# A gated delta-rule and FFN kernel: the first FFN group in plain f32, chunks 0 and 1 re-blocked by VectorE transposes, and a new order of the work

## The chip, the core and the metric

The kernel runs on one core of one Trainium2 chip. The metric is device time in microseconds (us) of one execution. The core has TensorE (PE, with its weight load PEld), VectorE (DVE), ScalarE (ACT), GpSimd (POOL), and SyncE (SP), which issues the DMAs here.

## The reference

```python
def _attn_ref(q, k, v, beta):                 # (4, 8, 768, 48) each, beta (4, 8, 768)
    k_n = k / (np.linalg.norm(k, axis=-1, keepdims=True) + 1e-06)
    state = np.zeros((B, H, D, D))
    for t in range(S):
        kt, vt, bt = (k_n[:, :, t], v[:, :, t], beta[:, :, t, None])
        y[:, :, t] = np.einsum('bhd,bhde->bhe', q[:, :, t], state)
        v_old = np.einsum('bhde,bhd->bhe', state, kt)
        state = state + bt[:, :, :, None] * np.einsum('bhd,bhe->bhde', kt, vt - v_old)
    return y

def _moe_ref(x, w_in, w_out):                 # x (3072, 384), w_in (384, 2048), w_out (2048, 384)
    h = x @ w_in
    sp = np.maximum(h, 0.0) + np.log1p(np.exp(-np.abs(h)))
    g = h * erf(sp)
    return g @ w_out
```

The rows of x are the 3072 tokens of y. The weights arrive as double precision numbers; the core sees each as two 32-bit integers.

## The kernel before, in words

**The recurrence.** The 768 steps are cut into 12 chunks of 64. For each chunk the kernel forms the norms of k (`norms`, L245 to L258, 18 small VectorE steps for two chunks), the Gram matrices k·k and q·k on TensorE (`gram_mm`, L287 for chunks 0 and 1, L291 later), their scaled or masked copies A and pp (`gram_a` L301, `gram_p` L308), and the inverse of a triangular matrix per head. That inverse is built from 32x32 blocks. Two chunks are solved together: A is written to DRAM (`to_dram` L328), read back with one block per partition (`to_blocks` L337, tile gb), and forward substitution runs in 31 rows of two elementwise steps (`solve_row`, L355 and L357), for chunks 0 and 1 on VectorE and later on POOL. The result xb goes back to matrix form: for chunks 0 and 1 by 256 small TensorE products with an identity matrix (`back_t` L373) and copies (`back_x`), later over DRAM (`put_blocks`, `from_blocks`). The 32x32 halves are merged (`merge_t` L405, a VectorE transpose into T; `merge_e`, `merge_z`, `merge_m`), and a chain over the four batches updates the state and gives y (`chain_u` L485, `chain_u2` L491, `chain_s` L499, `chain_s2` L504, `chain_y` L511/L515, `chain_y2`, `chain_m` L526).

**The weights.** Each weight matrix is loaded in pieces of 512 columns (`w_load` L558; 512 KB each) and turned into f32: `w_mask` (ACT, L565), `w_sign` (L572), `w_bits` (VectorE, L579), with a running maximum `w_mx` (ACT L587, VectorE L590). From the maximum comes a power-of-two scale; then each f32 tile of 384 columns becomes two f16 halves: `w_hi` (ACT, L130) and `w_lo` (L649 on VectorE; for w_in by TensorE f32 products with a scaled identity, L641 and L642, and an ACT copy).

**The FFN.** One group is 256 tokens, one chunk of all four batches: 12 groups. x is scaled and split into f16 halves (`x_max` to `x_lo`, L658 to L685). For each of 16 tiles of d_ff, `ffn1` issues nine f16 products of 256 columns (L697). In units of two tiles, `e_sp` (Softplus, L719), `e_erf` (L724, each behind a load of ACT's function table, L165) and `e_mul` (L728, reads the products of L697 from PSUM, tile ph) make g, which `e_split` (L123 on ACT or L125) and `e_rest` (L118) split into halves; `ffn2` issues six f16 products of 384 columns per tile (L749 to L751). `ffn_out` and `ffn_store` scale and store.

**Order.** A program is recorded as a list of events; the tuple `ORDER` says in which order they are issued and `ENG` on which engine an event with a choice runs. Each engine runs its own instructions in that order, and DMAs are issued by SP in that order too. Matmuls on zeros (`warm` L180, `fill2` L186) are put between the real ones.

## Time and profile before

| | |
|---|---|
| three runs | 611.24, 614.84, 613.77 us; median 613.77 us |
| profiled execution | span 613.8 us from first to last instruction; its own time is taken as the same, since the run of 613.77 us agrees with it to the digits shown |
| busy PE / DVE / ACT / POOL | 97% / 66% / 85% / 50% of the span |
| mean granted TensorE clock | 0.983 |
| first / last FFN product | starts at 96.05 / ends at about 608.5 us |

The span falls into two parts. Up to 96 us the first two chunks are prepared and the weights are read; from then on FFN products are issued until 608.5 us, with the recurrence of later chunks between them. A busy PE includes the products on zeros, so its 97% is not 97% of needed work.

### The profile page before, as it was taken

To read this page: it belongs to the slowest core of one execution; us is meant where nothing else is said; L and a number is where in the kernel's file an instruction comes from. 1 tells how busy PE (TensorE), PEld (TensorE's weight loads), DVE (VectorE), ACT (ScalarE), POOL (GpSimd) and SP (SyncE) were. 2 spreads that over 40 slices of the span, in tenths; PEclk is the share of its full clock that TensorE was granted. 3 is DMA by queue.
4 is the path that set the end of the run, shared out by engine and by line. 5 is a ranking of instruction groups with operands and counts; after the bars stand their busy time and mean duration, and the time that the engine had idled before them with its cause. 6 is when DMAs were issued, how large, how long until landed. Compare 5 with 4: busy or idle time off the path is not lost.

```text
span 613.8 us, 25249 instructions
## 1 busy us (share of the span) xinstructions
PE 595.4 (97%) x11019; PEld 426.9 (70%) x11019; DVE 403.8 (66%) x926; ACT 522.9 (85%) x751; POOL 307.8 (50%) x484
## 2 busy tenths in 40 slices
PE   9899989999999899999999999999999999999996
PEld 3654456667777677777777777777777777777773
DVE  0769986668787788887776977666565655436221
ACT  8859897999996789878968999897989797989873
POOL 3000313798589733998527884489953122213221
PEclk9799898999999899999999999999999999999999
DMA  9999625850755367624485226713045200100111
GB/s 313 281 235 350 152 52 124 226 141 28 185 105 142 93 163 153 156 63 117 92 212 140 67 66 148 148 50 91 1 115 121 53 17 21 27 2 14 27 27 26
DMA packets 86382, 69.72 MB, mean 114 GB/s; under 512 B 64064, under 2 KB 73408, under 8 KB 86272
## 3 DMA queue, kind: packets, MB, share of 16 engines
q1 hardware_dynamic: 86272, 68.12, 43.1%
q8 instruction: 86, 1.41, 1.0%
q14 instruction: 24, 0.20, 0.1%
HBM read 48.17 MB, written 18.87 MB: 109 GB/s over the span
## 4 chain that ended last, share of the span: by engine, by line
PE 72%; POOL 7%; DVE 5%; DMA 5%; ACT 5%; issue 4%; SPq 1%; POOLq 0%; DVEq 0%; ACTq 0%
PE ph L697 25%; PE pr L749 9%; PE pr L751 9%; PE pr L750 9%; PE warm L180 3%; POOL xb L357 3%; POOL tmptmpg L355 2%; PE pc L485 2%; DMA qp<-qT 2%; PE pc L511 2%; PE pm L448 2%; DMA k<-ktok 2%; PE pc L515 2%; PE pc L499 2%; PE pg L291 1%
## 5 line engine op out<-in xcount | busy, mean ns | idle before, releaser
L165 ACT ACT_TABLE_LOAD x169 | 216.8, 1283 | 3.0
L697 PE MATMUL ph<-xh,w_in 128*128 128x256 f16 x1152 | 206.8, 274 | 0.1
L697 PEld LDWEIGHTS <-w_in 128*128 128x128 f16 x1728 | 166.5, 98 | 30.5 <-issue 2.2
L697 PE MATMUL ph<-xl,w_in 128*128 128x256 f16 x576 | 157.8, 274 | 1.2 <-DVE xl L685 1.2
L118 POOL TENSOR_TENSOR H<-L,H 128x512 f16<-128x512 f32 x58 | 69.3, 1203 | 134.6 <-DVE H L125 89.8
L749 PE MATMUL pr<-w_out,H 128*128 128x384 f16 x384 | 126.1, 328 | 0.0
L750 PE MATMUL pr<-w_out,H 128*128 128x384 f16 x384 | 125.7, 327 | 0.0
L751 PE MATMUL pr<-w_out,H 128*128 128x384 f16 x384 | 125.7, 327 | 0.0
L728 DVE SCALAR_TENSOR_TENSOR L<-ph,L 128x512 f32<-128x512 f32 x96 | 65.8, 687 | 88.9 <-ACT L L724 74.7
L118 POOL TENSOR_TENSOR z<-v,nm 64x192 f32<-64x192 f32 x94 | 51.8, 551 | 99.9 <-DMA v<-vtok 86.0
L357 POOL TENSOR_TENSOR xb<-xb,tmptmpg 128x31 f32<-128x31 f32 (+15 forms) x154 | 90.7, 589 | 12.1
L355 POOL TENSOR_TENSOR tmptmpg<-gb,xb 128x31 f32<-128x31 f32 (+15 forms) x154 | 83.6, 543 | 24.4 <-DMA gb<-d 11.2
L719 ACT ACTIVATE L<-ph,xct 128x512 f32<-128x512 f32 x96 | 65.4, 687 | 29.3 <-PE ph L697 25.9
L724 ACT ACTIVATE L<-L 128x512 f32<-128x512 f32 x96 | 59.9, 629 | 0.9
L751 PEld LDWEIGHTS <-H 128*128 128x128 f16 x384 | 37.6, 98 | 25.1 <-issue 0.2
L749 PEld LDWEIGHTS <-H 128*128 128x128 f16 x384 | 37.5, 98 | 22.8 <-issue 0.2
L750 PEld LDWEIGHTS <-H 128*128 128x128 f16 x384 | 37.6, 98 | 20.2 <-issue 0.2
L180 PE MATMUL warm<-zero 128*128 128x512 f16 x192 | 49.5, 412 | 1.2 <-DVE zero L171 1.2
L491 DVE TENSOR_TENSOR z<-pc,ga 64x192 f32<-64x192 f32 x88 | 31.2, 355 | 18.1 <-PE pc L485 16.4
L123 ACT CAST H<-L 128x512 f16<-128x512 f32 x56 | 33.5, 610 | 8.0 <-DVE L L728 7.9
L504 DVE TENSOR_TENSOR z<-pc,z 48x192 f32<-48x192 f32 x80 | 28.3, 353 | 17.3 <-PE pc L499 14.0
L180 PEld LDWEIGHTS <-zero 128*128 128x128 f16 x192 | 18.9, 104 | 25.6 <-issue 7.2
(159 smaller groups left out, 857.1 us busy)
## 6 DMA issues: line engine op xcount, KB each, us to landing
raw_in<-w_in SPq DMA_DIRECT2D x12, 512.0 KB, 7.1
raw_out<-w_out SPq DMA_DIRECT2D x12, 512.0 KB, 6.5
d<-A SPq DMA_DIRECT2D x22, 256.0 KB, 3.4
d<-pp SPq DMA_DIRECT2D x10, 512.0 KB, 3.7
qp<-d SPq DMA_DIRECT2D x20, 256.0 KB, 4.9
k<-ktok SPq DMA_DIRECT2D x12, 384.0 KB, 4.9
kpg<-kT SPq DMA_DIRECT2D x24, 192.0 KB, 4.5
qp<-qT SPq DMA_DIRECT2D x24, 192.0 KB, 3.6
```

The costliest lines, as they stand in the source:

```text
L118: {"V": ve, "G": ge}[pick(d)].tensor_tensor(*a, **kw)
L165: se.add_instruction(mybir.InstLoadActFuncSet(name=nc.get_next_instruction_name(), act_func_set_id=i, ins=[], outs=[]))
L180: te.matmul(wp[0], zero[:, :P], zero, start=True, stop=True)
L355: eng.tensor_tensor(tv, G[:, s, s + 1:].unsqueeze(1).broadcast_to([P, ncol, nr]), Xv[:, :, s:s + 1].broadcast_to([P, ncol, nr]), op=ALU.mult)
L357: eng.tensor_tensor(Xv[:, :, s + 1:], Xv[:, :, s + 1:], tv, op=ALU.add)
L697: te.matmul(ph, w[:, i, kt * P:kt * P + P], G[x][:, :, ksl], start=(m == 0), stop=(m == 8))
L719: se.activation(unit(g, u), G["ph", u], AF.Softplus, bias=0.0, scale=G["ct"])
L724: se.activation(Lu, Lu, AF.Erf, bias=0.0, scale=1.0)
L728: ve.scalar_tensor_tensor(Lu, fg[g]["ph", u], HSC, Lu, op0=ALU.mult, op1=ALU.mult)
L749: te.matmul(G["po"][a], gh[:, o, asl], wout_h[:, i, :], start=(i == 0), stop=False)
L750: te.matmul(G["po"][a], gh[:, o, asl], wout_l[:, i, :], start=False, stop=False)
L751: te.matmul(G["po"][a], gl[:, o, asl], wout_h[:, i, :], start=False, stop=(i == NFF - 1))
```

## The change

**FFN group 0 in f32** (`GF=1`). Group 0 multiplies y and the rebuilt f32 weights directly: three f32 products of 256 columns per tile in `ffn1` (L866), two of 384 columns per tile in `ffn2` (L925), `e_mul` without the scale (L903), no `e_split`, `e_rest`, x scale or x halves. Both halves of the weights are made behind that (events of `parts`), `w_lo` always on VectorE (L819) and not by TensorE. The halves of a tile lie over the f32 values of the tile before it, so `w_hi` of tile i waits for group 0's products of tile i-1. w_in has two scales (first four tiles, and the rest).

**Blocks of chunks 0 and 1.** The way over DRAM is replaced by three strided VectorE transposes (`block_t`, L491), the way back by two transposes (`back_t`, L520) and copies; `merge_t` for these chunks reads A in place.

**Order and engines.** `ORDER` and `ENG` are new. The solve rows of all chunks are shared between VectorE and POOL (VectorE 73 pairs of 186, before 31); norm steps of later chunks go to POOL; A and pp of later chunks are copied by ACT and multiplied by POOL or VectorE. Memsets of xm and z go from ACT to POOL. The tag of ph has three PSUM buffers (before two) and pr two (before three). 300 products on zeros of 384 columns (before 192 and 63 of 512).

```diff
-ORDER = (1321,1,1276,1266,2,3,4,5,6,7,8,9,10,11,12,
+ORDER = (0, 1, 24, 27, 28, 16, 19, 22, 14, 11, 7, 5, 2,
...
-LPE = ("in",)
+RI = {"in": "EH", "in2": "EHLHLHLH"}
+NA = 4
+LPE = {"in": (), "out": ()}
+GA, GP = (2, 3, 4, 5), (0, 1, 2, 3, 4, 5)
+PN = (1, 2, 3, 4, 5)
...
+WF = 300
+GF = 1
...
-    ps1 = ctx.enter_context(tc.tile_pool(name="ps1", bufs=2, space=bass.MemoryType.PSUM))
+    ps1 = ctx.enter_context(tc.tile_pool(name="ps1", bufs=3, space=bass.MemoryType.PSUM))
...
+    def block_t(k):
+        if 0 not in gb_t:
+            gb_t[0] = at.tile([P, 32, 32], F32, tag="gb", name="gb0")
+        q, f = (slice(0, P), 1) if k == 0 else (slice((k - 1) * C, (k - 1) * C + 32), 0)
+        ve.transpose(gb_t[0][q].rearrange("p s t -> p t s"), A01[q].rearrange("p c a x -> p (c a) x")[:, :, f * 32:f * 32 + 32].rearrange("p m t -> p t m"))
...
-        for t in range(k * 8, k * 8 + 8):
-            for th in range(2):
-                for f in range(2):
-                    q0, p0 = i * 64 + f * 32, th * 64 + f * 32
-                    te.matmul(s["bt"][th][p0:p0 + 32, :, t], xb_t[sg][q0:q0 + 32, :, th * 16 + t], ident[q0:q0 + 32, q0:q0 + 32], start=True, stop=True)
...
+    def back_t(k):
+        ve.transpose(half(k).rearrange("p x t -> p t x"), xb_t[0][:, :, k * 16:k * 16 + 16].rearrange("p i j -> p j i"))
...
-    def w_lo1(nm, i):
-        a, h, _ = w_parts(nm, i)
-        ps = wt[nm]["ps", i] = pr[i % PB][:, :DM]
-        te.matmul(ps, ids[nm], a, start=True, stop=False)
-        te.matmul(ps, idn, h, start=False, stop=True)
...
+    def w_lo(nm, i):
+        a, h, l = w_parts(nm, i)
+        if i in LPE[wn[nm]]:
+            cp("A", l, wt[nm]["pl", i])
+            return
+        ve.scalar_tensor_tensor(l, a, w_sc(nm, i), h, op0=ALU.mult, op1=ALU.subtract)
...
+        if g < GF:
+            for kt in range(3):
+                te.matmul(ph, stage("in", i * DM + kt * P, P), ygrp[g][:, :, kt * C:kt * C + C], start=(kt == 0), stop=(kt == 2))
+            return
...
+        if g < GF:
+            for a in range(GS // 2):
+                te.matmul(G["po"][a], unit(g, u)[:, o, a * P:a * P + P], stage("out", i * DM, DM), start=(i == 0), stop=(i == NFF - 1))
+            return
...
+    for c in range(NC_):
+        if c == GF:
+            parts()
```

The following pieces show where the order moved instructions. First SP's queue, from its first DMA. raw_in are pieces of w_in, k and kpg the keys (by token, and by feature), be is beta. Before:

```order
L558 DMA raw_in_117<-w_in 128x1024
L558 DMA raw_in_120<-w_in 128x1024
L558 DMA raw_in_122<-w_in 128x1024
L208 DMA k_198<-ktok 128x768
L275 DMA kpg_200<-kT 48x1024 x2
L558 DMA raw_in_213<-w_in 128x1024
L558 DMA raw_in_219<-w_in 128x1024
L208 DMA k_223<-ktok 128x768
```

and with the change:

```order
L288 DMA k_127<-ktok 128x768
L294 DMA be_133<-btok 128x32
L288 DMA k_135<-ktok 128x768
L393 DMA kpg_147<-kT 48x1024 x2
L393 DMA kpg_150<-kT 48x1024 x2
L722 DMA raw_in_243<-w_in 128x1024
L722 DMA raw_out_245<-w_out 128x1024
```

The keys of both chunks moved ahead of all weights. Next VectorE, from the last scaled Gram matrix to the first solve row (tmp of gb and xb), before:

```order
L301 TENSOR_TENSOR w_out<-pg_0_284,gn_237 128x512
L579 SCALAR_TENSOR_TENSOR w_in<-w_in,raw_in_384 128x512
L579 SCALAR_TENSOR_TENSOR w_in<-w_in,raw_in_117 128x512
L590 TENSOR_REDUCE mx_in<-raw_in_393 128x1
L579 SCALAR_TENSOR_TENSOR w_in<-w_in,raw_in_393 128x512
L308 TENSOR_TENSOR pp_439<-pr_81,mask 128x512
L579 SCALAR_TENSOR_TENSOR w_in<-w_in,raw_in_391 128x512
```

(18 more of these kinds and of the scale of w_in stand before the first L355) and with the change:

```order
L430 TENSOR_TENSOR w_out<-pg_1_226,gn_259 128x512
L491 STREAM_TRANSPOSE gb_282<-w_out 128x32x32
L491 STREAM_TRANSPOSE gb_282<-w_out 32x32x32 x2
L507 TENSOR_TENSOR tmp_0_286<-gb_282,xb_223 128x31
L509 TENSOR_TENSOR xb_223<-xb_223,tmp_0_286 128x31
L507 TENSOR_TENSOR tmp_1_289<-gb_282,xb_223 128x60
```

The solve follows the transposes at once; the weights' rows moved between and behind the solve rows. Last VectorE around the halves of group 1's x (xl), with the change:

```order
L787 TENSOR_SCALAR c_out<-c_out,m_out 128x1
L819 SCALAR_TENSOR_TENSOR w_in<-w_in,sc_in_114 128x384
L855 SCALAR_TENSOR_TENSOR xl_2125<-y_1593,xsx_1879,xh_2124 128x384 x2
L212 TENSOR_TENSOR A_2128<-A_2128,gn_1801 128x512 x2
L903 TENSOR_TENSOR L_3_1977<-ph_7_1947,L_3_1977 128x512
L212 TENSOR_TENSOR A_2020<-A_2020,gn_1801 128x512
L819 SCALAR_TENSOR_TENSOR w_out<-w_out,sc_out 128x384
L743 SCALAR_TENSOR_TENSOR w_out<-w_out,raw_out_1346 128x512
L819 SCALAR_TENSOR_TENSOR w_in<-w_in,sc_in_114 128x384
```

Here the last unit of group 0 (L903), the lower halves of both weights (L819) and rebuilt bits of w_out (L743) stand together. Before, only rows of `w_lo` of w_out stood around group 1's xl; no `w_bits` row and no row of w_in followed it.

## Rows read from the trace of the kernel before

**Rows 1.** Page: busy time, share of the span and instructions of each engine.

```profile
PE 595.4 (97%) x11019; PEld 426.9 (70%) x11019; DVE 403.8 (66%) x926; ACT 522.9 (85%) x751; POOL 307.8 (50%) x484
```

**Rows 2.** Windows: stretch, busy time (and count) of PE, PEld, DVE, ACT, POOL, PEclk, DMA share, GB/s.

```profile
96.00:202.00 106.00, 102.20 (x2112) 71.75 (x2107) 77.92 (x164) 94.91 (x133) 80.91 (x131) 0.98 0.56 139
202.00:280.00 78.00, 75.45 (x1852) 59.19 (x1852) 64.99 (x154) 65.84 (x92) 50.67 (x87) 0.98 0.52 129
280.00:608.60 328.60, 328.40 (x5638) 244.63 (x5636) 190.80 (x420) 283.44 (x364) 162.05 (x241) 1.00 0.29 70
```

**Rows 3.** DMA over 0 to 20 us: bandwidth in slices of half a microsecond.

```profile
GB/s 0 0 0 131 115 311 360 418 401 401 393 393 365 373 410 342 215 229 246 229 303 369 410 393 428 391 410 451 410 426 401 410 459 401 426 401 361 279 229 246
```

**Rows 4.** Chain of waits from the start: start us, us, what.

```profile
4.94 9.32 DMA k<-ktok
```

**Rows 5.** Timeline of DVE, first block solve and what surrounds it: start, us, engine, instruction.

```profile
15.36 0.95 DVE L234 TENSOR_REDUCE n<-sq 128x16 f32<-128x768 f32 x1 [0.89 <-ACT sq L226]
...
16.34 0.18 DVE L245 TENSOR_SCALAR n<-n 128x32 f32<-128x32 f32 x1
...
16.56 0.18 DVE L247 TENSOR_SCALAR ri<-n 128x32 int32<-128x32 int32 x1
...
24.47 0.69 DVE L301 TENSOR_TENSOR A<-pg,gn 128x512 f32<-128x512 f32 x1
...
42.18 0.18 DVE L355 TENSOR_TENSOR tmpT<-gb,xb 128x31 f32<-128x31 f32 x1
...
66.26 0.22 DVE L357 TENSOR_TENSOR xb<-xb,tmpT 128x60 f32<-128x60 f32 x1
...
70.46 0.70 DVE L405 STREAM_TRANSPOSE T<-xm 32x512 f32<-32x512 f32 x1
...
90.89 0.87 DVE L526 TENSOR_REDUCE mg<-y 128x1 f32<-128x192 f32 x3
```

**Rows 6.** Timeline of POOL, last row of the first solve.

```profile
67.27 0.60 POOL L357 TENSOR_TENSOR xb<-xb,tmpT 128x31 f32<-128x31 f32 x1
```

**Rows 7.** Timeline of PE: first product of the FFN, some of its products, the last.

```profile
96.05 0.28 PE L697 MATMUL ph<-xh,w_in 128*128 128x256 f16 x1
...
300.34 0.38 PE L697 MATMUL ph<-xh,w_in 128*128 128x256 f16 x2
...
300.67 0.38 PE L697 MATMUL ph<-xh,w_in 128*128 128x256 f16 x2
...
607.89 0.33 PE L749 MATMUL pr<-w_out,H 128*128 128x384 f16 x1
...
608.22 0.33 PE L751 MATMUL pr<-w_out,H 128*128 128x384 f16 x1
```

**Rows 8.** Chain of waits, 48 to 51 us: f32 products of 384 columns.

```profile
49.27 0.65 PE pr L641 x2
```

**Rows 9.** Windows just behind the first product (columns as in rows 2).

```profile
98.00:101.00 3.00, 3.00 (x18) 1.92 (x20) 0.66 (x1) 1.92 (x3) 1.24 (x3) 0.50 0.27 91
```

**Rows 10.** Groups by line, 96 to 202 us: busy us, mean ns of one, idle before.

```profile
L165 ACT ACT_TABLE_LOAD x32 | 41.1, 1283 | 0.6
...
L649 DVE SCALAR_TENSOR_TENSOR w_out<-w_out,sc_out 128x384 f16<-128x384 f32 x16 | 12.0, 752 | 3.0 <-ACT w_out L130 2.9
...
L118 DVE TENSOR_TENSOR H<-L,H 128x512 f16<-128x512 f32 x8 | 9.2, 1162 | 0.0
...
L186 PE MATMUL pr<-zero 128*128 128x512 f16 x63 | 15.8, 381 | 0.0
...
L123 ACT CAST H<-L 128x512 f16<-128x512 f32 x15 | 8.8, 610 | 0.0
```

**Rows 11.** Timeline of DVE and POOL: one step alone, and one beside POOL.

```profile
121.80 0.61 DVE L649 SCALAR_TENSOR_TENSOR w_out<-w_out,sc_out 128x384 f16<-128x384 f32 x1
...
130.12 1.44 DVE L649 SCALAR_TENSOR_TENSOR w_out<-w_out,sc_out 128x384 f16<-128x384 f32 x1
...
129.98 1.16 POOL L118 TENSOR_TENSOR H<-L,H 128x512 f16<-128x512 f32 x1
```

More of the change, by code (lines that the diff above doesn't have):

```diff
@@ L626, in w_hi, with w_sc @@
+    def w_parts(nm, i):
+        v = wv[wn[nm]]
+        return stage(nm, i * DM, DM), v[:, i, 0, :], v[:, i, 1, :]
+    def w_sc(nm, i):
+        return wt[nm]["sc"] if nm != "out" else wt[nm]["sc"][:, part(i):part(i) + 1]
+    def w_hi(nm, i):
         a, h, _ = w_parts(nm, i)
-        scaled("A", h, a, wt[nm]["sc"])
+        scaled("A", h, a, w_sc(nm, i))
+    idn = con.tile([P, P], F16, name="idn")
+    ids = [con.tile([P, P], F32, name=f"ids{i}") for i in range(2)]
     def w_ident():
         ve.tensor_scalar(idn, ident, -1.0, None, op0=ALU.mult)
-    def w_idsc(nm):
-        ve.tensor_scalar(ids[nm], ident, wt[nm]["sc"], None, op0=ALU.mult)
@@ L852, in delta_ffn_kernel @@
-    on(us(31.5), load_kf, 3, "qpg")
+            on(put_p, c)
+            for h in range(2):
+                on(to_dram, c, h)
+    on(clear_first)
+    on(clear_second)
+    for i in range(2):
+        for hb in range(2):
+            on(clear_q, i, hb)
+    for i in range(2):
+        for hb in range(2):
+            on(clear_x, i, hb)
+    for i in range(6):
+        on(clear_z, i)
+    on(load_beta, 0)
+    on(load_mask)
+    on(load_ident)
+    for c in range(2):
+        on(load_step, c)
+        on(load_kf, c, "kpg")
+        on(load_q, c)
+        prep(c)
@@ new lines, in delta_ffn_kernel, with parts @@
+            on_p(c, i)
+        on(put_p, c)
+    for nm in tags:
+        for i in range(len(cut[nm])):
+            on(w_load, nm, i)
+            on(w_mask, nm, i)
+            on(w_sign, nm, i)
+            on(w_bits, nm, i)
+            on(w_mx, nm, i)
+    def parts():
+      for nm in tags:
+        on(w_max, nm)
+        on(w_all, nm)
+        on(w_scale, nm)
+        if nm == "in":
+            on(w_ident)
+        for p in range(2):
+            if any(part(i) == p for i in LPE[wn[nm]]) and (nm == "out" or p == list(RI).index(nm)):
+                on(w_idsc, nm, p)
+        for i in range(*{"in": (NA,), "in2": (NA, NFF), "out": (NFF,)}[nm]):
+            on(w_hi, nm, i)
+            if i in LPE[wn[nm]]:
+                on(w_pe, nm, i)
+            on(w_lo, nm, i)
@@ new lines, in delta_ffn_kernel @@
+        g = c
+        if g >= GF:
+            on(x_max, g)
+            on(x_all, g)
+            on(x_scale, g)
+            on(x_scale2, g)
+            for i in range(GS // 2):
+                on(x_hi, g, i)
+                on(x_lo, g, i)
+        for u in range(NFF // EU):
+            for i in range(EU):
+                on(ffn1, g * NFF + u * EU + i)
+            for fn in (e_sp, e_erf, e_mul, e_split, e_rest)[:3 if g < GF else 5]:
+                on(fn, g, u)
+            for i in range(EU):
+                on(ffn2, g * NFF + u * EU + i)
```

602 lines of the change are left out of this document (256 added, 346 removed), and 117 rows, old and new, of tables (ENG, ORDER).

## The prediction

> **What bounds the kernel now.** I read the page first, then windows, then the chain and the engines' timelines at the places that the change touches. The page [rows 1] gives PE 97% busy, but that counts the products on zeros, so the stages must be read apart. From 280 us on PE is busy 328.40 of 328.60 us at clock 1.00 [rows 2]: real work without a gap, and the change adds or removes hardly anything there. The FFN's first product starts at 96.05 and the last ends at 608.22 + 0.33 = 608.55 [rows 7]; the 5.2 us of scale and store behind it stay. So the end is the start of the FFN, plus PE's needed work, plus what PE loses. It loses in two places. Before 96 us the span is a chain of latencies: the second k lands at 4.94 + 9.32 = 14.26 [rows 4], the first multiply into A runs at 24.47, the first solve row only at 42.18 and the last VectorE row at 66.26 [rows 5], POOL's at 67.27 [rows 6]. From 96 to 202 us PE is busy 102.20 of 106 [rows 2], but 15.8 of it is 63 products on zeros [rows 10], and 98 to 101 run at clock 0.50, the 1.2 GHz level [rows 9]. About 3.8 + 15.8 + 1.5 = 21 us are lost there.
>
> **Step 1: the FFN starts earlier.** I go along the new path by durations of the old one.
> - Data. k, beta and k of chunks 0 and 1 (784 KB) lead the queue. By the slices of half a microsecond, 668 KB are through at 4.0 and 868 KB at 4.5 [rows 3], so they are there at 4.3. From landing to the end of the second sum it took 16.31 - 14.26 = 2.05 [rows 4, 5]: 6.5, taken as 7 for hand-offs.
> - Norms: 18 steps at 0.22 from start to start [rows 5], now with no weights' row between them: 4.1, so 11.1. Four multiplies into A at 0.69 [rows 5], overlapping by a tenth: 2.4, so 13.5.
> - Blocks. The DMA trip and the weights' rows that stood beside it go: 17.7 us lie between the first multiply into A and the first solve row, at 24.47 and 42.18 [rows 5]. In their place are three strided transposes of 1024 elements per partition. The nearest row is a transpose of 512 in 0.70 [rows 5], 1.36 ns each: 4.2, so 17.7. No row shows a strided one; bounds are this price and four times it (rival E).
> - Solve: 42.18 to 66.48 less 1.5 for two rows of weights between = 22.8. POOL's last pair, 1.3 with its hand-off [rows 6], stays. Six pairs go to POOL, where a step of 31 elements takes 0.60 against 0.18 [rows 5, 6]; on longer ones I take 0.25 more, as an estimate between none and that: 12 steps and a hand-off, 3.2. Rows of weights between: 1.9, one mask product and one copy: 1.3; hand-offs between engines: 1.5. Sum 32, so 49.7.
> - Back: 0.7 for the second transpose (the first lies under POOL rows), 0.4 a copy, 1.4 for T: 52.2. The 256 small products go.
> - Then the merge and the chain of four batches. Before, T ended at 70.46 + 1.4 = 71.89 and the first FFN product came at 96.05 [rows 5, 7], 24.2 later. In f32 it needs no scale: the stretch from the end of the last maximum, 90.89 + 0.87 = 91.76 [rows 5], to 96.05 goes (4.3). 19.9 is left: **72**, a gain of **24**. Bounds: if the weights' rows that now stand there cost 0.6 each on this path for ten of them, 18; if the chain itself tightens as the weights' maxima leave it, 28.
>
> **Step 2: f32 products cost more.** An f32 product of 384 columns takes 0.65 [rows 8]; one of 256 by columns 0.433. 48 and 32 of them: 20.8 + 20.8 = 41.6. In f16 group 0 took 144 at 0.109 (three in 0.33) and 96 at 0.165 (two in 0.33) [rows 7]: 31.4. **+10.2**. The 16 f32 products that made w_in's lower halves go too, but they lay under the solve: 0.
>
> **Step 3: what PE loses behind the start.** The stretch of 106 us, by engine:
> - ACT was busy 94.91 [rows 2]. By ACT's order 22 table loads instead of 32 stand between the first Softplus and the first of group 2, since group 0's units are issued in batches: 10 x 1.283 = 12.8 less [rows 10]. Eight casts of group 0 go, 0.61 each [rows 10]: 4.9 less. Sixteen upper halves of w_in come in, 0.5 each by that cast's length (384 columns of 512): 8 more, about 85.
> - VectorE was busy 77.92 [rows 2]. In come 11 more lower halves at 0.65 (7.2), 14 rows of bits (8.5) and 8 maxima (4.9) at 0.61 as an elementwise step alone [rows 11], 34 solve steps at 0.38, the mean of the first solve (22.8 over 60; 12.9): 33.5. Out go eight `e_rest` of 9.2 [rows 10] and about 3 of x halves and norms: about 99.
> - PE needs 102.2 - 15.8 + 10.2 = 97.
>
> So the stretch, 106 + 10.2 = 116 if nothing else changed, has three engines between 85 and 99. If they fit together perfectly it shrinks to 100, x = -16; VectorE becomes the tightest, and its rows stand in one order: where group 1's halves wait for rows of w_out's bits, or `w_hi` of a tile waits for group 0's last use of the tile before, PE waits with it. I take x = **-3**, nearer to today's loss than to none, since VectorE at 99 of 113 is fuller than PE's own need was (86 of 106). Ends: -15 and +12.
>
> **Sum.** 613.8 - 24 + 10.2 - 3 = **597**, against the profiled execution; its 613.8 is the median of the runs to the digit, so nothing is added.
>
> **Other edits.** Memsets on POOL: POOL is idle in most of the first 40 us, 0. Norms, A and pp of later chunks on POOL and ACT: from 280 on ACT has 283 busy of 328 and POOL 162 [rows 2], hidden. Three ph buffers: they let PE run one unit ahead, in x.
>
> **Rivals.**
> - **B. PE alone binds.** ACT's relief counts fully, VectorE's rows find gaps: x = -15, 613.8 - 24 + 10.2 - 15 = 585. For: ACT was the fuller of the two before [rows 2]. Against: VectorE would have to be busy 99 of 101.
> - **C. VectorE and POOL get in each other's way.** A lower half took 0.61 alone and 1.44 with POOL's step beside it, mean 0.75 [rows 10, 11]. With POOL sharing solve rows with VectorE and multiplying A and pp, the 27 lower halves, 34 solve steps and 24 multiplies and rests in the stretch would each cost more, by the mean 0.14, with more such pairs 0.18: 85 x 0.18 = 15, x = +12 instead of -3, 612, or **609** where a fifth of it falls into gaps, which I take. The Trainium skill (SBUF — State Buffer, SBUF: two separate sides) says why: a VectorE step with two inputs from SBUF and a GpSimd step lock one port pair, and the later one blocks fully. The trace agrees in part: the step that took 1.44 had 1.02 of POOL's step still ahead of it and lost 0.83. By that rule the change, which puts more such pairs side by side, loses time.
> - **D. Slower: group 0 runs at the 1.2 GHz level.** Place: the f32 group, from its first product on. In [rows 9], 2 us behind the first product, 18 products take 3.0 us at clock 0.50. With f32 products that come one tile at a time, as bits arrive, PE has gaps all through the group. All at the low level: 41.6 more, 638. It decides from 18 us (43% of the group at the low level): then 597 + 18 = 615, no gain. Against: the order has 300 products on zeros for these gaps, and in the same stretch of before the clock was 0.98 [rows 2].
> - **E. Strided transposes are four times as long.** The five cost 5.6 by the price above (three of 1.4, two of 0.7); four times that is 22.4, all on the path: 597 + 16.8 = 613.8, no change. No row speaks for it or against it; the whole gain of step 1 would have to be eaten by five instructions of 4.5 on average against the 0.70 seen, so it gets the smallest chance.
>
> **How the numbers follow.** Forecast 597: chance 0.54; B 0.20; C 0.14; D 0.08; E 0.04. Predicted time 597. The range 579 to 615 takes B with 6 us of error of the start, the bounds of step 1 (18 to 28) and of x, C and E; D is left out, and some of the rest. A measurement of this kernel can tell 0.5% from no change, 610.7 to 616.9. Faster by more: the forecast, B, most of C: 0.79. Within: E, the rest of C, the edge of the forecast: 0.12. Slower: D and mishaps of its size: 0.09.
>
> **What would show it.** On the timeline of VectorE the first solve row should stand near 18, the transposes at 1.4 each, the end of T near 52; PE's first product of L866 near 72, with 0.43 and 0.65 per product, at a granted clock near 1. In the window from that product over 116 us PE's products on zeros should have gone, VectorE be busiest, and `w_lo` be near 0.7 on average. It is wrong if the start comes after 80 (solve or transposes), if group 0's window shows a clock under 0.8 (D), if `w_lo` and solve rows on VectorE run at over 1 us on average (C), or if from 280 us on PE is no longer without gaps.

## The result: 1.1% slower, and the profile after

The changed kernel takes 618.04 us (median of 8 runs, 616.93 to 620.17), the kernel before 610.85 us in the same session (8 runs, 608.26 to 614.84): ratio 1.0107, 95% interval 1.0075 to 1.014. The forecast was 597, in a range of 579 to 615, with a chance of 0.09 for slower: wrong in sign and outside the range.

The profiled execution took 618.54 us with a span of 616.6, so 1.9 us lie around the span. The profile of before has a span of 613.8. Wherever the record lists both, a run of before takes 1.7 to 1.9 us more than its span, so its profiled execution took about 615.6 us, more than any of its eight runs; that the span agreed with a run of 613.77 us was chance. The two traces therefore differ by 2.8 us only, the medians by 7.2. What follows accounts for the 2.8.

The clock may hold a part of the other 4.4. The profiled execution of before has a mean granted clock of 0.983; in the six sessions that followed, the median of before's runs is 0.991 to 0.993, and the eight runs of the changed kernel have a median of 0.981. Among 32 of the 34 runs of before in the session of e1 (two long ones left out), the nine at a clock of 0.995 or more took 610.6 us on average and the eight at 0.987 or less 615.5. Clock and time go together here; that the clock makes the 4.4 us is not shown.

The page's busy times of the changed kernel, to be read against [rows 1]:

```profile
PE 584.7 (95%) x10680; PEld 427.7 (69%) x10680; DVE 458.6 (74%) x1022; ACT 441.8 (72%) x628; POOL 271.1 (44%) x463
```

ACT lost 81 us of work, VectorE gained 55. Windows with the columns of [rows 2]: before from its first FFN product to the first of group 2; then the changed kernel from its first FFN product to the first of group 2, to 280 us, and to its last product.

```profile
96.00:206.70 110.70, 105.93 (x2192) 74.21 (x2187) 80.17 (x168) 97.58 (x138) 83.50 (x135) 0.97 0.55 134
```

```profile
77.00:187.60 110.60, 105.68 (x2102) 76.53 (x2099) 99.34 (x230) 94.81 (x150) 63.58 (x108) 0.98 0.61 146
187.60:280.00 92.40, 90.67 (x1844) 68.49 (x1841) 76.21 (x159) 65.74 (x93) 61.66 (x113) 1.00 0.58 136
280.00:608.70 328.70, 324.00 (x5636) 240.37 (x5634) 216.24 (x487) 243.89 (x322) 111.39 (x181) 0.99 0.29 63
```

From 280 us on PE was without gaps before (328.40 of 328.60); now 4.7 us are missing there. And the FFN starts 19 us earlier, but its last product ends at 608.7 as it did before (608.5).

The next table is worked out from every product in PE's trace: each counts from its start to the start of the next, or to its own end if that comes first; the rest is idle. FFN is both layers, recurrence every other real product. All times are in us, and those of FFN, recurrence, zeros and idle are counted from the first FFN product to the end of the last.

```
                  FFN starts  FFN    recurrence  zeros  idle  last ends  tail  span
before               96.0    387.2     103.3     15.4    6.5    608.5    5.2   613.8
changed              77.0    398.9     103.9     17.5   11.3    608.7    7.9   616.6
difference          -19.0    +11.7      +0.6     +2.1   +4.8             +2.7   +2.8
forecast            -24      +10.2               -3 together              0    -16.8
```

By the same count, zeros and idle together rose by 2.3 us up to 280 us (21.8 to 24.1) and by 4.6 behind it (0.1 to 4.7). The lead of 19 us is still on the clock when group 2's first layer starts, at 187.6 against 206.7, but less of the second layer is done by then: that of group 1 starts at 191.9, in before at 175.9.

**The start.** VectorE's timeline up to the second transpose into T:

```profile
7.28 0.95 DVE L314 TENSOR_REDUCE n<-sq 128x16 f32<-128x768 f32 x1 [1.45 <-ACT sq L306]
8.27 0.40 DVE L325 TENSOR_SCALAR n<-n 128x32 f32<-128x32 f32 x1
8.70 0.89 DVE L327 TENSOR_SCALAR ri<-n 128x32 int32<-128x32 int32 x1
9.63 0.89 DVE L328 TENSOR_SCALAR ri<-ri 128x32 int32<-128x32 int32 x1
...
13.87 0.18 DVE L338 TENSOR_SCALAR ga<-gn 128x32 f32<-128x32 f32 x1
...
16.47 6.10 DVE L491 STREAM_TRANSPOSE gb<-w_out 128x1024 f32<-128x1024 f32 x3
22.68 0.19 DVE L507 TENSOR_TENSOR tmp<-gb,xb 128x31 f32<-128x31 f32 x1
...
51.98 1.14 DVE L520 STREAM_TRANSPOSE gb<-xb 128x512 f32<-128x512 f32 x1 [0.72 <-POOL xb L509]
...
53.80 1.43 DVE L550 STREAM_TRANSPOSE T<-xm 32x512 f32<-32x512 f32 x2 [0.23 <-ACT xm L217]
```

and POOL's rows beside the norm steps, and at the end of the solve:

```profile
7.68 0.95 POOL L268 MEMSET qp<- 128x1024 f32 x1
8.57 1.91 POOL L271 MEMSET xm<- 128x1024 f32 x2
...
51.67 0.27 POOL L509 TENSOR_TENSOR xb<-xb,tmp 128x31 f32<-128x31 f32 x1
```

The strided transposes take 2.03 each on average, not 1.4. The first is on 128 partitions, the other two on 32, and all three take about the same. Three norm steps take 0.40, 0.89 and 0.89 instead of 0.18; the first and the last of them end 0.04 us behind the end of a memset (8.63 and 10.48). The solve runs from 22.68 to 51.94, 29.3 us where 32 were forecast. T is ready at 55.23 and the first product comes 21.8 us later.

**The stretch behind it.** The groups of the changed kernel from 77 to 193 us:

```profile
L265 PE MATMUL pr<-zero 128*128 128x384 f16 x89 | 18.5, 348 | 0.0
L819 DVE SCALAR_TENSOR_TENSOR w_in<-w_in,sc_in 128x384 f16<-128x384 f32 x15 | 10.5, 700 | 0.2 <-ACT w_in L224 0.2
...
L819 DVE SCALAR_TENSOR_TENSOR w_out<-w_out,sc_out 128x384 f16<-128x384 f32 x12 | 8.0, 663 | 0.2
```

Up to group 2's start VectorE was loaded as forecast (99.34 of 110.6 us, where 99 of 113 was written), but ACT was not relieved: 94.81, where about 85 was written and before stood at 97.58. Its table loads fell from 33 to 22, as forecast (42.3 to 28.2 us); what the forecast's sum did not hold is 9.8 us for bits and maxima of the weights (L729, L736, L751) and 4.6 us for copies of A and pp (L217). The lower halves cost 0.70 and 0.66 us, no more than the 0.75 of [rows 10]. The products on zeros have not gone: 89, for 17.5 us of PE.

**A new stall at 311 to 322 us.** VectorE, then POOL, then PE:

```profile
311.07 4.38 DVE L855 SCALAR_TENSOR_TENSOR xl<-y,xsx,xh 128x384 f16<-128x384 f32 x2 [0.46 <-ACT xh L224]
317.58 0.19 DVE L507 TENSOR_TENSOR tmp<-gb,xb 128x31 f32<-128x31 f32 x1 [2.14 <-issue]
...
320.96 0.69 DVE L905 SCALAR_TENSOR_TENSOR L<-ph,L 128x512 f32<-128x512 f32 x1
```

```profile
311.12 3.38 POOL L212 TENSOR_TENSOR H<-L,H 128x512 f16<-128x512 f32 x3
```

```profile
318.81 0.55 PE L630 MATMUL pc<-z,xm 128*32 128x48 f32 x32 [0.83 <-DVE z L649]
321.70 0.37 PE L871 MATMUL ph<-xh,w_in 128*128 128x256 f16 x1 [2.35 <-DVE L L905]
```

The two xl steps take 4.38 together, 3.85 of it the first, which ends only once POOL's three rests are through (314.50). The Trainium skill (SBUF — State Buffer, SBUF: two separate sides) says that a VectorE step with two inputs from SBUF and a GpSimd step which reads SBUF exclude each other for a whole instruction. The trace agrees, and here the step waited out three such instructions in a row. Behind xl stands the first solve row of chunks 8 and 9 (L507), which waits for its blocks to come back from DRAM. The chain of waits names that transfer:

```profile
311.81 3.63 DMA gb<-d
315.44 2.14 issue
```

SP issued this transfer behind a load of k (L288) and one of v (L608) that had itself waited 1.3 us in SP's queue. Whether an earlier issue alone would remove the stall was not run. For the 2.14 us between the landing and the row the profile shows no cause.

In before, POOL ran nearly all later rows, and POOL waited. Now VectorE waits, with `e_mul` (L905) queued behind, and PE waits for that unit's PSUM. PE lost 3.2 us in two waits, and then the clock fell:

```profile
300.00:320.00 20.00, 18.21 (x411) 12.55 (x410) 13.21 (x28) 14.16 (x23) 5.96 (x10) 1.00 0.76 148
320.00:340.00 20.00, 18.30 (x410) 14.03 (x410) 15.24 (x35) 12.18 (x16) 13.46 (x23) 0.83 0.07 19
```

**The tail** grew from 5.2 to 7.9 us. The output tile in before, and the output tile and its stores in the changed kernel:

```profile
608.59 0.62 DVE L132 TENSOR_SCALAR ob<-pr,xco 128x384 f32<-128x384 f32 x1 [4.42 <-PE pr L751]
```

```profile
608.75 0.62 DVE L226 TENSOR_SCALAR ob<-pr,xco 128x384 f32<-128x384 f32 x1 [10.21 <-PE pr L932]
609.39 4.60 SPq L946 DMA_DIRECT2D out<-ob  x6
612.25 0.62 DVE L226 TENSOR_SCALAR ob<-pr,xco 128x384 f32<-128x384 f32 x1 [2.88 <-DMA out<-ob]
```

The last `ob` waits 2.88 us for a store: ob has two buffers, and the store of group 10 is issued only among those of group 11.

### The profile page after: what moved, and what is told of

Its sections match the earlier page's. It is cut to its first block, busy times and chain, and to the rows that moved or that the text cites. A ratio compares the mean times of both kernels' runs of the same rounds, so it can differ in the third digit from the quotient of the medians.

```text
span 616.6 us, 24419 instructions
## 1 busy us (share of the span) xinstructions
PE 584.7 (95%) x10680; PEld 427.7 (69%) x10680; DVE 458.6 (74%) x1022; ACT 441.8 (72%) x628; POOL 271.1 (44%) x463
## 4 chain that ended last, share of the span: by engine, by line
PE 69%; DVE 17%; ACT 4%; DMA 3%; issue 3%; POOL 2%; SPq 0%; DVEq 0%; ACTq 0%; POOLq 0%
PE ph L871 25%; PE pr L930 9%; PE pr L932 8%; PE pr L931 8%; PE pc L630 3%; PE pr L925 2%; DVE tmp L507 2%; PE pc L656 2%; DVE xb L509 2%; PE pc L644 2%; PE ph L866 2%; PE pm L593 2%; PE pc L660 1%; PE pg L409 1%; PE pe L561 1%
## 5 line engine op out<-in xcount | busy, mean ns | idle before, releaser
L871 PE MATMUL ph<-xh,w_in 128*128 128x256 f16 x1056 | 191.4, 275 | 2.3 <-DVE L L905 2.3
L871 PEld LDWEIGHTS <-w_in 128*128 128x128 f16 x1584 | 152.5, 99 | 30.1 <-issue 4.0
L871 PE MATMUL ph<-xl,w_in 128*128 128x256 f16 x528 | 145.1, 275 | 0.9 <-DVE xl L855 0.9
L930 PE MATMUL pr<-w_out,H 128*128 128x384 f16 x352 | 115.1, 327 | 0.0
L931 PE MATMUL pr<-w_out,H 128*128 128x384 f16 x352 | 114.8, 326 | 0.0
L932 PE MATMUL pr<-w_out,H 128*128 128x384 f16 x352 | 114.8, 326 | 0.0
L212 POOL TENSOR_TENSOR H<-L,H 128x512 f16<-128x512 f32 x39 | 46.2, 1192 | 132.6 <-ACT H L217 64.5
L507 POOL TENSOR_TENSOR tmp<-gb,xb 128x255 f32<-128x255 f32 (+14 forms) x113 | 62.3, 551 | 80.4 <-DVE xb L509 69.1
L905 DVE SCALAR_TENSOR_TENSOR L<-ph,L 128x512 f32<-128x512 f32 x88 | 59.4, 685 | 51.4 <-ACT L L898 51.0
L509 POOL TENSOR_TENSOR xb<-xb,tmp 128x255 f32<-128x255 f32 (+14 forms) x113 | 64.7, 572 | 8.9
L265 PE MATMUL pr<-zero 128*128 128x384 f16 x300 | 59.4, 352 | 1.2 <-DVE zero L261 1.2
L212 POOL TENSOR_TENSOR z<-v,nm 64x192 f32<-64x192 f32 x66 | 35.5, 537 | 54.1 <-DMA v<-vtok 30.8
L636 DVE TENSOR_TENSOR z<-pc,ga 64x192 f32<-64x192 f32 x94 | 33.4, 355 | 15.0 <-PE pc L630 12.7
L212 DVE TENSOR_TENSOR H<-L,H 128x512 f16<-128x512 f32 x49 | 37.2, 770 | 1.5 <-ACT H L217 1.3
```

What stands on the lines that cost most here:

```text
L212: {"V": ve, "G": ge}[pick(d)].tensor_tensor(*a, **kw)
L265: te.matmul(pr[1][:, :DM], zero[:, :P], zero[:, :DM], start=new, stop=new)
L507: eng.tensor_tensor(tv, g.unsqueeze(1).broadcast_to([P, ncol, nr]), Xv[:, :, s:s + 1].broadcast_to([P, ncol, nr]), op=ALU.mult)
L509: eng.tensor_tensor(Xv[:, :, s + 1:], Xv[:, :, s + 1:], tv, op=ALU.add)
L871: te.matmul(ph, w[:, i, kt * P:kt * P + P], G[x][:, :, ksl], start=(m == 0), stop=(m == 8))
L905: ve.scalar_tensor_tensor(Lu, fg[g]["ph", u], HSC, Lu, op0=ALU.mult, op1=ALU.mult)
```

## Experiments

All are edits of the changed kernel unless said otherwise; ratios are against before in the same session. An interval is about ±0.3%, or 2 us, and the unedited kernel gave 1.0107 in one session and 1.0067 in another, so effects under 3 us are read from the traces. The FFN's start also moved between traces, from 77.0 to 80.3, with edits that do not touch what lies ahead of it, so places of group 1 and group 2 are given behind it. Group 0, 1 or 2 "starts" with the first product of its first layer.

**The unedited kernel again (c_after), the control.**

> The changed kernel itself, as control on the same chip as the three runs that follow: a ratio to before of 1.007 to 1.014 by the first measurement. A second profile also shows what of the first was chance: the start of the FFN at 77 to 79, the stall of about 3 us near 320 us and a tail of 7.9 us should come back, single stretches at clock 0.50 need not.

616.56 us, 1.0067 (1.0039 to 1.0096). The FFN starts at 78.2 and its last product ends at 607.8; zeros take 17.7, idle time 10.6 and the tail 7.8; the stall at 320 is there again, with a wait of 2.35 us.

**The late store (e1_store).** In `ORDER`, `ffn_store(10, 0)` moves right behind its `ffn_out`.

```diff
 2101,
+2102,
...
-2102,
```

> Theory (tail): in the changed kernel the last result tile waits 2.88 us for a store of group 10 that SP issues only behind a store of group 11, since both share an ob buffer; the tail behind the last product is 7.9 us instead of 5.2. With that store moved to its own result tile, the tail is 5.2 again, both last ob steps within 1.5 us behind the last product, and the time is 2.7 lower than the changed kernel's (ratio to before near 1.006). Rival (the stores' own landing sets the tail): the tail stays at 7.5 to 8 and the ratio at 1.011.

615.46 us, 1.0026 (0.9995 to 1.0057). The tail is 5.7 us instead of 7.9: the cause is shown, for 2.2 us.

**The waiting solve row (e2_row0).** The first rows of chunks 8 and 9, and 10 and 11, go back to POOL.

```diff
-1596: 'V',
...
-1938: 'V',
```

> Theory (a wait put into VectorE's queue): the first solve rows of chunks 8/9 and 10/11 wait for the blocks that come back from DRAM, and since they stand on VectorE, the state update, the merge and a unit's multiply behind them wait too; PE stalls 3.2 us near 320 us and then runs 6.8 us at clock 0.50, which costs 3.4 more. With these two rows on POOL, no stretch at clock 0.50 lies between 300 and 340, PE is idle there for under 1 us, and the time is 5 to 7 lower than the changed kernel's (ratio near 1.000). Rival (the lead would be lost in the next wait anyway, because PE waits for VectorE's load): the stall moves, and the time is lower by under 2.

616.02 us, 1.0054 (1.0028 to 1.0081). Windows of this kernel, and its longest wait of the weight load:

```profile
300.00:320.00 20.00, 19.98 (x435) 13.93 (x436) 15.67 (x36) 14.39 (x23) 3.23 (x4) 1.00 0.83 152
320.00:340.00 20.00, 17.73 (x483) 14.22 (x482) 14.68 (x34) 15.13 (x21) 17.02 (x29) 0.99 0.23 62
```

```profile
339.12 2.97 PEld L871 LDWEIGHTS <-w_in 128*128 128x128 f16 x17 [2.50 <-DVE L L905]
```

The stall at 320 goes, so row 0 on VectorE made it; one of the same size comes at 339, where the first row of this solve that VectorE still has (128x247) waits 3.99 us for the row before it on POOL. A shared solve in a fixed order hands the wait on.

**More solve rows on POOL.** e10_pool345 puts all rows of chunks 6 to 11 on POOL, e11_pool12345 all of chunks 2 to 11 (entries of `ENG` taken out, as above).

> All solve rows of chunks 6 to 11 on POOL, as before the change. With only the first rows there, the wait at 320 us went and one of 2.5 us came at 339, where a solve row on VectorE waits 4.0 for POOL's. Theory (solve rows that pass from POOL to VectorE and back hold up VectorE's queue, and with it PE): PE is idle for under 1.5 us between 300 and 400, and the time falls by 2 to 4 against the control. Rival (POOL alone solves too slowly for this order, and the merge of a chunk waits instead): idle time of PE in 300 to 400 stays at 3 or more, no gain or a loss.

> All solve rows of chunks 2 to 11 on POOL: VectorE is relieved of 17 pairs (11 us) in the stretch from 77 to 193 us, and POOL gets them at about twice the time. Theory (VectorE's load with its hand-offs is the cost of sharing the rows): a gain of 2 to 6 against the control. Rival (sharing is needed so that chunks 2 and 3 are solved in time): the start of group 2's first layer moves from 189 to 195 or later, and the time rises by 3 or more.

620.9 us, 1.0119 (1.008 to 1.0157), and 626.81 us, 1.0199 (1.0126 to 1.0272). Window 340 to 380 us of e10:

```profile
340.00:380.00 40.00, 34.30 (x658) 25.50 (x656) 21.34 (x50) 27.20 (x35) 32.27 (x63) 0.87 0.31 75
```

POOL alone is too slow for these rows: PE loses 5.7 us here and the clock falls. In e11 group 2 starts 119.1 us behind the FFN's first product, against 111.2 in the control: a longer solve of chunks 2 and 3 holds it back. Both rivals were right: sharing the rows is needed in this order.

**Memsets beside the norms (e3_memset).** The memsets of xm (events 8 and 6) move behind a later POOL step.

```diff
-8,
-6,
...
 396,
+8,
+6,
```

> Theory (memsets on POOL hold up VectorE's one-input steps): in the changed kernel three norm steps take 0.40, 0.89 and 0.89 us instead of 0.18, each ending with a memset on POOL. With the two memsets of xm behind the first products of v, the last two take 0.18 and 0.18 to 0.40, the solve starts 1.4 us earlier than 22.68, and the FFN's first product about 1.4 earlier than 77.0; the time falls by 0 to 1.4. If the lock also holds up transposes, one of the block transposes grows by up to 1 us each for two memsets. Rival (these steps are slow for their integer operands): they stay at 0.89.

616.41 us, 1.0049 (1.0009 to 1.0088). VectorE:

```profile
8.69 0.18 DVE L327 TENSOR_SCALAR ri<-n 128x32 int32<-128x32 int32 x1
8.91 0.18 DVE L328 TENSOR_SCALAR ri<-ri 128x32 int32<-128x32 int32 x1
...
13.89 0.69 DVE L430 TENSOR_TENSOR w_out<-pg,gn 128x512 f32<-128x512 f32 x1 [1.26 <-PE pg L405]
15.50 0.69 DVE L430 TENSOR_TENSOR w_out<-pr,gn 128x512 f32<-128x512 f32 x1 [0.92 <-PE pr L405]
```

The steps fall from 0.89 to 0.18 and the norms end 1.4 us earlier, but the Gram products then come last (1.26 and 0.92): the first solve row stands at 23.64, against 22.68 and 23.72 without the edit. The collision is real and hidden.

**All three (e4_all), and the tail with the last tile on ACT (e14_tail).** e14 is e1 and e3, and the second `ob` of group 11 on ACT instead of VectorE.

> All three edits together. If the three are separate places of the path, the gains add: 2.7 + 6 + 1 = 10, 608 against the changed kernel's 618 and a ratio to before of 0.995. Rival (one shared limit behind them, VectorE's load): the sum is smaller than the largest single gain plus 2, ratio 1.00 to 1.005.

> The changed kernel with the late store of group 10 moved to its tile, the two memsets of xm moved, and the last result tile's scale left to ScalarE instead of VectorE. Theory: the tail behind the last product is 5.2 to 5.4 instead of 7.9, the start is as in the control, and the time is 2.5 to 3.5 below the control's: a ratio to before of 1.001 to 1.004, level with before, not ahead of it. Rival: the tail stays at 5.7, ratio 1.003 to 1.006.

613.98 us, 1.002 (0.9988 to 1.0052), and 614.78 us, 1.000 (0.9968 to 1.0032). e4's ratio lies where its rival put it (1.00 to 1.005): the three gains do not add up to 10 us. The last tile on ACT brought nothing (a tail of 5.65 in e14, 5.66 in e1), as its rival said. Both are level with before, not ahead of it.

**The keys first, alone (e5_keysfirst).** Before's kernel, with k, beta and the Gram operands loaded ahead of five pieces of w_in, and the norm steps following them; `ORDER` only.

> The kernel before with one part of the change alone: the keys and beta of chunks 0 and 1 are issued ahead of the five pieces of w_in that led SP's queue, and the norm steps follow at once. Theory (the first 42 us are a chain of latencies that starts with the keys): the second sum of squares ends near 7 to 9 instead of 16.3, the first solve row starts 5 to 9 us earlier than 42.18, and the FFN's first product 3 to 8 earlier than 96.05; the time falls by 2 to 6 if the lead is kept to the end, by under 1 if a later stage gives it back. Rival (the weights, now two microseconds later, set the start of the FFN): the start moves by under 1.

614.71 us, 1.0026 (0.9979 to 1.0072). The sums of squares end at 11.6 instead of 16.3, but the first solve row gains 2.6 us only (39.55, against 42.18 in [rows 5]) and the FFN's start about 1. The first multiply into A stands at 24.94 (24.47 in [rows 5]): the early keys wait already ahead of it, before the way to the blocks begins.

**VectorE's halves (e6_zerolo).**

```diff
-        ve.scalar_tensor_tensor(l, a, w_sc(nm, i), h, op0=ALU.mult, op1=ALU.subtract)
+        ve.memset(l, 0.0)
```

> Leaves out the computation of all 32 lower halves of the weights: they are set to zero, which should take VectorE about 0.2 us each instead of 0.68, 14 us less in all, some 12 of it between the FFN's first product and 193 us; nothing waits for the upper halves any more there. Theory (VectorE's queue bounds the stretch from 77 to 193, where it was busy 103 of 116 us and PE lost some 23 to products on zeros and waits): the last product of group 1's first layer comes 6 to 10 us earlier, and the time falls by 5 to 9 against the control. Rival (PE's own work, with the f32 products, bounds it): under 2.

616.5 us, 1.0066 (1.0033 to 1.01). Group 1 starts 57.8 us behind the FFN's first product instead of 61.0, group 2 at 109.3 instead of 111.2; the last product ends at 606.7 against the control's 607.8. VectorE's maximum of y for group 2 and the reduce of its spread, in the control and in this kernel:

```profile
179.50 0.16 DVE L828 TENSOR_REDUCE xm<-mg 128x1 f32<-128x4 f32 x1
...
181.32 0.28 DVE L835 TENSOR_REDUCE xm<-sp 128x1 f32<-128x128 f32 x1
```

```profile
172.99 0.16 DVE L828 TENSOR_REDUCE xm<-mg 128x1 f32<-128x4 f32 x1
...
176.19 0.95 DVE L314 TENSOR_REDUCE n<-sq 128x16 f32<-128x768 f32 x1 [2.44 <-ACT sq L306]
178.27 0.29 DVE L835 TENSOR_REDUCE xm<-sp 128x1 f32<-128x128 f32 x1 [1.13 <-PE sp L707]
```

With VectorE relieved the maximum comes 6.5 us earlier, the reduce 3.05 and group 2 about 2. Between the first two VectorE's queue holds a sum of squares for keys of a later chunk (L314), for which it waits 2.44 us on ACT, and the spread's product on PE (L707) comes late as well. So VectorE's load does count up to y, and the order gives most of that back.

**No products on zeros (e7_nofill).** The 89 behind the first FFN product leave `ORDER`.

> The 89 products on zeros behind the FFN's first product are left out (17.5 us of PE's time). Theory: they fill waits for VectorE, so PE is idle instead, the time changes by less than 2 either way, or rises by up to 4 if the clock falls to 0.50 more often. Rival (they stand in the way of needed products): the time falls by 4 or more.

622.5 us, 1.0162 (1.0112 to 1.0211). Windows 78 to 139 and 139 to 193 us, of the control, then of this kernel:

```profile
78.00:139.00 61.00, 57.87 (x1046) 41.88 (x1035) 53.14 (x136) 50.95 (x81) 33.97 (x61) 0.97 0.67 168
139.00:193.00 54.00, 51.85 (x1187) 37.69 (x1185) 48.40 (x104) 47.01 (x74) 32.26 (x50) 1.00 0.47 111
```

```profile
78.00:139.00 61.00, 48.70 (x958) 38.04 (x955) 52.28 (x128) 49.74 (x80) 33.11 (x61) 0.92 0.69 173
139.00:193.00 54.00, 49.24 (x1080) 35.49 (x1081) 47.47 (x109) 45.09 (x75) 28.63 (x46) 0.91 0.50 110
```

17.7 us of zeros go; 12.4 come back as idle, and at clock 0.92 and 0.91 the real products cost 10.1 us more (FFN 405.3 against 397.8, recurrence 106.1 against 103.5). The rise is more than the 4 us that the theory allowed; 2.1 of it lies ahead of the FFN, whose start is at 80.3 in this trace. The zeros cover waits; taking them out makes the waits dearer.

**Less PE work (e8_onekt), both cuts (e9_both).** Of three f32 products per tile in group 0's first layer one is left; e9 is e6 and e8.

```diff
-            for kt in range(3):
-                te.matmul(ph, stage("in", i * DM + kt * P, P), ygrp[g][:, :, kt * C:kt * C + C], start=(kt == 0), stop=(kt == 2))
+            te.matmul(ph, stage("in", i * DM, P), ygrp[g][:, :, :C], start=True, stop=True)
```

> Leaves out two of the three f32 products per tile in group 0's first layer: 32 products of 0.433, 13.9 us of PE's work less. Theory (VectorE bounds the stretch to 193 us): most of it turns into idle time, and the time falls by 2 to 5. Rival (PE's f32 work bounds it, so that the 10 us by which f32 costs more come back in full): the time falls by 10 to 14.

> Both cuts of the runs that zeroed the lower halves and that left out two of three f32 products of group 0's first layer (it leaves out both). Alone, neither changed the time by more than 2, though the first moved the start of group 1's first layer from 139.2 to 135.9 and the second ended group 0's first layer 5 earlier. Theory now (VectorE with ACT, and PE, are both full in this stretch, and each alone holds it): together the start of group 1's first layer comes 8 us or more earlier than 139.2. The time then falls by 5 or more if PE keeps that lead, or by under 2 if what follows (the recurrence of chunks 2 to 5, in the order given) holds it back. Rival (a third thing holds group 1's start, such as the rebuilt weights' arrival): its start stays within 1 us of 135.9.

618.6 us, 1.0085 (1.0055 to 1.0115): 12.7 us less of FFN products, 9.8 more idle, 1.5 more zeros, 2.1 more for the recurrence, no gain. e9: 615.51 us, 1.0062 (1.0025 to 1.01); group 1 at 56.9, group 2 at 107.4 behind the start, last product at 603.5 in its trace, whose execution of 613.31 us was one of its faster ones. The FFN's products take 15.1 us less than in the control (382.7 against 397.8) and a lower half 0.22 us instead of 0.66 to 0.70, but only 4.1 us come back at group 1 and 3.8 at group 2: the loads of the two pace the stretch in a small part at most.

**A shorter solve (e12_shortsolve), three cuts (e13_three).** Rows 9 to 18 of chunks 2 and 3 return at once; e13 adds e9.

```diff
+        if sg == 1 and 9 <= s <= 18: return
```

> Leaves out ten of the 31 solve rows of chunks 2 and 3 (rows 9 to 18, all on POOL, 15 us in the control). Theory (three chains of nearly equal length to 190 us: PE's queue, VectorE's with ACT's, and the solve of chunks 2 and 3 with its trips over DRAM): alone it gains little; group 2's first layer starts 0 to 4 us earlier than 189.4 and the time falls by 0 to 4 against the control. Rival (this solve alone holds the FFN back): group 2 starts 8 to 15 earlier and the time falls by 8 or more.

> All three cuts together: lower halves zeroed, two of three f32 products of group 0's first layer left out, ten solve rows of chunks 2 and 3 left out. Theory: with all three chains shorter, group 2's first layer starts 8 us or more earlier than 189.4 (the first two cuts alone left it within 4), and the last product ends 8 or more earlier than 607.8, unless the recurrence of chunks 4 and 5 holds it next. Rival (a fourth thing): within 3 us of what the first two cuts gave.

617.24 us, 1.0015 (0.9978 to 1.0052), and 617.53 us, 1.003 (0.9986 to 1.0073). Group 2 starts 113.0 and 110.1 behind, the control's at 111.2. The row behind the ten, on VectorE, in the control and in e12:

```profile
122.83 0.39 DVE L507 TENSOR_TENSOR tmp<-gb,xb 128x240 f32<-128x240 f32 x1
```

```profile
122.92 0.40 DVE L507 TENSOR_TENSOR tmp<-gb,xb 128x240 f32<-128x240 f32 x1
```

It does not move, since it stands in VectorE's queue behind the maximum of y and a unit's multiply. The work of the ten rows goes, and POOL is idle in its place, but the solve ends no earlier (56.2 us behind the start, 55.1 in the control). So these rows do not hold group 2, and what a solve that ends earlier would give is not tested by either run.

**ScalarE (e15_act), and all three engines (e16_all3).** Group 0 without Erf and with a copy for Softplus, so without a dozen table loads; e16 adds e9.

```diff
+        if g < GF:
+            se.activation(unit(g, u), G["ph", u], AF.Copy, bias=0.0, scale=1.0)
+            return
...
+        if g < GF: return
```

> Edit: group 0 of the FFN leaves out Erf, and its Softplus is a plain copy from PSUM on ScalarE, so that the dozen table loads and the Erf steps (about 15 + 5 us of ScalarE between the FFN's start and group 1's) are gone; everything else stays. Left out: the two functions of group 0. What is told apart: group 1's first product came 61 us behind the FFN's first in the control, 58 with VectorE's lower halves thinned, 57 with PE thinned as well. Theory, ScalarE holds it: it was busy 51 of those 61 us, so group 1 starts 50 us behind the FFN's first product or sooner, and the time is 5 to 10 us under the control's, 606 to 611 beside a before of 612. Rival, it is held by the chain that makes chunk 1's y and its halves, or by PE: group 1 starts 59 to 61 behind, and the time stays within 2 us of the control's, 615 to 617.

> Edit: ScalarE's cut of the run before (no Softplus, Erf or table loads in group 0) together with the two cuts already tried jointly (all lower halves of the weights set to zero by memsets in place of the two-input step, and one f32 product of three in group 0's first layer). Left out: as said. With PE, VectorE and ScalarE all relieved, group 1's first product came 57 us behind the FFN's first with two of them. If the engines' loads bound this stretch, it now comes at 45 to 50, and the time is 598 to 606 beside a before of 612; if the chain of chunk 1's y and x halves binds, it stays at 55 to 57 and the time at 613 to 616.

616.55 us, 1.0076 (1.0043 to 1.011), and 617.88 us, 1.0061 (1.0016 to 1.0106). Window 78 to 139 us of e15:

```profile
78.00:139.00 61.00, 58.73 (x1042) 42.55 (x1036) 54.13 (x138) 32.13 (x63) 33.96 (x61) 0.97 0.67 166
```

19 us of ACT's work are gone (50.95 to 32.13), and group 1 starts at 60.1; with all three cuts it starts at 57.8, and PE's idle time is 21.8 in all. Cutting the loads takes 3 or 4 of the 61 us and leaves the rest.

**The order (e17_xearly), on top of e14.** Group 1's chain moves up in `ORDER`: spread and scale of x (430, 431), halves (433 to 436), first tile (437, 438), the last units of group 0 (288, 308, 309), the first Softplus (439); 14 zeros behind the old place of 430 go.

```diff
 285,
+430,
+431,
...
 287,
+433,
+435,
...
 588,
+434,
+436,
+288,
...
 275,
+437,
+438,
```

> Edit, on top of the run with the tail mended: in the recorded order, the spread, the scale and the halves of group 1's x move from behind chunks 2 and 3's solve rows and group 0's last products to right behind the maximum of y; group 1's first tile, Erf and the product of group 0's last unit move up with them, ScalarE's first Softplus of group 1 moves ahead of three weight steps, and 14 products on zeros that stood in this gap go. Theory, the recorded order sets group 1's start (12 us lie between the maximum of y and the reduce that uses its spread, while VectorE and PE go through other rows): group 1 starts 54 to 57 us behind the FFN's first product instead of 61, and the time falls by 2 to 4 us against the kernel with the tail mended, to 0.993 to 0.998 of before. Rival, the time is given back at the next wait (halves of w_out, Softplus of group 1, the start of group 2): group 1 starts earlier, but the last FFN product stays within 1.5 us of the control's 607.8 and the ratio within 0.998 to 1.004.

616.12 us, 1.0059 (1.0024 to 1.0093). VectorE's maximum of y, the reduce of its spread, and the halves, in the control and in this kernel:

```profile
122.16 0.14 DVE L828 TENSOR_REDUCE xm<-mg 128x1 f32<-128x4 f32 x1
...
134.00 0.28 DVE L835 TENSOR_REDUCE xm<-sp 128x1 f32<-128x128 f32 x1
...
137.81 1.14 DVE L855 SCALAR_TENSOR_TENSOR xl<-y,xsx,xh 128x384 f16<-128x384 f32 x2
```

```profile
122.28 0.14 DVE L828 TENSOR_REDUCE xm<-mg 128x1 f32<-128x4 f32 x1
...
125.40 0.28 DVE L835 TENSOR_REDUCE xm<-sp 128x1 f32<-128x128 f32 x1
...
131.43 1.14 DVE L855 SCALAR_TENSOR_TENSOR xl<-y,xsx,xh 128x384 f16<-128x384 f32 x2
```

Group 1 starts 56.0 us behind the first product instead of 61.0 (60.8 in e14): the recorded order held it by 4.8 us. The 2.0 us of zeros that go with the edit do not explain that, since e8 took 12.7 us off PE and moved group 1 by 0.7. But group 2 starts at 189.2, in e14 at 188.6, and the last product ends at 606.9 against 607.9: the rival was right, the lead is given back before group 2. Its ratio is above what both had written. (The ratios of e14 and e17 come from two sessions and their intervals overlap; whether the edit costs anything they don't tell.)

## Why the prediction was wrong, step by step

The forecast sum gave a span of 597, and 616.6 was measured. Of the 19.6 us between them, 5.0 come from the start, 2.1 from f32 products and the recurrence, 5.3 from what PE loses up to 280 us, 4.6 from what it loses behind, and 2.7 from the tail.

- **Step 1, the start: right in kind, 5.0 us short** (19.0 of 24, inside its bounds of 18 to 28). The sums end at 8.23 instead of 7; norms take 5.8 instead of 4.1, beside memsets that the text set at 0 because POOL was idle there (e3 shows this hidden behind the Gram products in any case); transposes 6.2 instead of 4.2; the way back to T 3.3 instead of 2.5; the chain behind T 21.8 instead of 19.9. The solve was 2.7 better than forecast, so part of the agreement is luck: the other terms were late by 7.7.
- **Step 2, f32 products: right.** +10.2 was written; both layers together grew by 11.7, with the products that ran at the 1.2 GHz level among them.
- **Step 3, what PE loses: the step that failed.** x was -3; up to 280 us zeros and idle together rose by 2.3 instead. Its premise was that ACT's relief lets the stretch shrink towards PE's need. The relief itself came to 2.8 us and not to 10. And a relief does little there: e6, e8, e9, e15 and e16 relieved VectorE, PE and ACT, alone and together, and group 1 kept 57 to 60 us behind the FFN's start, group 2 107 to 110 (61 and 111 in the control), with no gain in the time. So for the most part the stretch is paced not by busy time but by waits between engines that each go through a fixed order. Three places of it are seen: in e17 a new order, with 14 zeros fewer, brings group 1 forward by 4.8; in e12 a row of the solve stays where it was though the ten ahead of it are gone; in e6 VectorE's lead at y ends in a row that waits for ACT. What would bring group 2 forward, and with it the time, stays open: a longer solve of chunks 2 and 3 holds it back (e11), a shorter one was not reached, and neither that nor the rest of their recurrence was moved in the order.
- **"Hardly anything" from 280 us on: wrong too.** 4.7 us of gaps stand there, most of them in the stall at 311 to 322, and a clock stretch. The order showed VectorE 73 pairs of rows where it had 31; the step asked what they cost, not what the first of them waits for and what is queued behind it (e2). That moved wait is a rival which was not written. Gaps behind 280 us were named as a sign of a wrong prediction, and they came.
- **The tail, taken as unchanged: +2.7.** A store far behind its tile in SP's order (e1).

Of the rivals, E has the right direction only: strided transposes at 1.5 times, not 4. C's collision shows beside the norms and in one larger place (4.38 for two halves of x, 1.14 elsewhere), while the lower halves of the weights on average got no dearer. D's mechanism is there in small: two stretches at the 1.2 GHz level, 3.4 us behind the FFN's start and 6.8 at 321, where before has 3.4 us behind the FFN's start and 3.4 at 203. The zeros keep it small: without them (e7) the two windows run at 0.92 and 0.91. B falls with e8, e9 and e16.

No version tried beats the kernel before. The best measured, e14, is level with it.

## What to carry to other kernels

In a kernel whose engines each run a fixed order, busy shares do not tell what a relief is worth: find the step that the next stage's first instruction waits for, and go back through each queue to what stands ahead of it. An instruction that is moved to a busier engine brings its wait along, so ask of its first input, above all where that comes over DRAM, when it lands and what then stands behind it. And a change of order wants its last 10 us read too: one store out of place cost 2.2 us here. When a cut of work gains nothing, look whether the next row moved at all: in e12 it did not, and the cut then tells little about what was cut.
